# Reordering the first weight loads of a fused attention and MLP kernel, with a new issue order to go with it

## The chip, the cores and the metric

The kernel runs on one core of one Trainium2 chip. The metric is the device time of one execution in microseconds (us). The time before is the median of 11 executions.

## The reference

One input `x` (2048 tokens by 512 features, bfloat16) is layer-normed once to `xn`, and both branches read `xn`; the result is the sum of `x` and the two branches.

- Branch A: q, k and v are `xn @ wq`, `xn @ wk`, `xn @ wv`, split into 32 heads of 16 features. The 2048 tokens are cut into four segments of 512. In each segment every head does causal softmax attention inside the segment, and also reads a memory: with `phi(t) = t + 1` for positive t and `exp(t)` otherwise, the memory output is `phi(q) @ M / (phi(q) @ z)`. After the segment, `M += phi(k).T @ v` and `z += sum(phi(k))`. A sigmoid gate per head (`beta`) mixes the two, and the result goes through `wo`.
- Branch B: `silu(xn @ w1) @ w2` with 1792 hidden features.

```python
x = A_x
xn = _layernorm(x, axis=-1)
return x + _A_ref(xn, A_wq, A_wk, A_wv, A_wo, A_beta) + _B_ref(xn, B_w1, B_w2)
```

## The kernel before

The work is cut into tasks, and each task is a few instructions on one engine: a DMA issue on SyncE's queue (`"SP"`) or ScalarE's queue (`"ACTQ"`), matmuls on TensorE (PE), activations on ScalarE (ACT), vector work on VectorE (DVE), masks and small products on GpSimd (POOL). `Sched.add` makes a task with its engine, an assumed duration, an assumed delay until its result can be seen (`vis`), what it depends on and which buffers it takes. `Sched.run` then goes through the string `ORDER`, a list of task numbers written out by hand or by a search outside the kernel, and emits the tasks in that order. So the order of the instructions on every engine is `ORDER`; nothing is decided on the chip except the waits. `run` also keeps track of assumed times, and it uses them for one choice: which buffer of a ring a task gets.

The parts that matter here:

- **First loads.** `load_x` (line 369) and `load_w` (line 381) issue one DMA each. The first segment's four row tiles of `x` (128 tokens each) go out first, two on each queue. The weights `w_k` and `w_q` are loaded in two halves of 256 columns (256 KB each); the first halves serve the first two head groups. `w_v` is one load of 512 KB; `w_1` comes in two halves of 896 KB. The weights are loaded once and stay.
- **Warm-up.** 26 tasks of two small matmuls on an identity keep PE occupied until real work is there.
- **Layer norm of the first segment** (`ln`, line 546): for each row tile statistics on DVE (tile 2 on ACT), a power on POOL, the normalisation on DVE into `xn`, four transposes on PE (line 630) and a copy into `xnT` by ACT (line 643), or by DVE for tile 3 (line 645).
- **First projections.** `first_tile` (line 691) makes k and q of head group 0 in pieces, as row tiles come in: 128-column pieces for tiles 0 and 1, a 256-column piece for tiles 2 and 3. From a k piece ACT makes one half of `kB` (line 721) and DVE the other (line 723); DVE also keeps `kT` (line 731). `v_tile` (line 796) makes v for one row tile with four 512-column matmuls, and DVE evicts it to `V` (line 807).
- **The long middle.** `quad` (line 847) is one of 72 score groups: up to 16 small matmuls on 32-row tiles of PE write four PSUM banks `psS`, one ACT exponential over 2048 columns (line 870) reads them, and POOL masks the result (line 889). There is a single `psS`, so a score group waits for the exponential before it. Between two score groups PE does other work: projections, `w_1` and `w_2` matmuls, the probability-times-v products (`pv`), `w_o`.
- **The tail** (`tail`, line 1237): after the last score group the remaining `w_2` and `w_o` matmuls of the last segment, the last normalisation, and the stores.

All matmuls go through one helper, line 504 of the profile.

Of the kernel before, what the change touches and what calls it, by code (L numbers as in the profile page):

```python
# [64 lines left out]
1 3 5 14 27 0 2 53 63 28 29 15 30 31 32 64 33 54 34 4 35 36 58 55 37 38 39 40 41 42 65 59 60  # L65
43 44 45 66 70 46 71 47 56 57 48 49 50 51 67 61 62 72 52 96 109 16 6 110 68 69 97 111 7 8 9
10 98 73 74 18 114 115 99 17 116 11 112 113 100 117 19 147 101 102 184 118 103 136 129 12 130
185 131 187 148 149 132 137 150 104 105 138 188 189 268 269 270 139 76 75 271 272 13 151 133
280 106 281 282 283 140 77 284 78 84 124 273 186 192 125 107 285 126 127 193 143 81 128 274
275 82 276 277 119 120 121 122 21 123 135 196 168 278 279 169 170 108 83 171 194 172 286 287  # L70
288 289 163 164 197 142 141 190 200 79 298 299 300 301 292 80 293 290 294 85 295 291 134 86
199 201 302 87 165 89 166 167 204 152 153 154 296 297 155 328 198 329 330 202 331 205 156 179
303 203 90 180 173 332 333 88 208 209 181 191 195 182 159 144 145 304 158 305 157 160 183 220
222 221 210 212 213 306 307 161 352 353 354 355 356 214 215 358 308 309 382 383 384 385 216
217 310 311 312 386 206 313 314 363 364 146 315 428 429 430 357 431 175 226 227 211 365 366
367 432 316 317 318 319 207 218 320 22 321 371 372 373 374 230 671 219 672 673 674 223 231
375 228 176 234 177 433 225 368 235 675 229 434 224 91 435 436 420 437 174 421 390 391 178
376 392 393 237 92 238 239 322 323 324 325 326 422 394 443 444 445 236 446 377 676 423 424
241 242 243 438 439 327 440 369 447 441 20 240 359 334 335 336 337 442 338 339 677 678 246
247 401 402 403 404 405 232 340 360 341 342 343 346 347 348 349 93 450 23 233 250 679 361 244  # L80
680 344 345 350 351 94 245 409 410 411 412 413 251 248 370 262 264 254 487 252 488 406 407
489 572 162 451 452 453 454 455 456 457 458 459 460 461 462 463 464 465 466 397 255 256 253
580 490 263 467 491 258 259 257 492 362 681 493 494 517 689 690 691 692 693 495 249 496 571
587 588 398 497 498 260 499 261 579 581 682 518 519 694 500 425 501 520 399 400 582 589 387
521 583 522 523 524 388 590 591 265 266 449 469 584 448 683 592 684 685 573 686 687 525 389
595 526 527 596 267 695 696 697 24 698 502 574 426 427 585 528 529 530 531 599 688 503 594
504 593 505 597 701 702 703 704 506 408 470 471 699 700 395 577 578 507 600 602 705 508 603
872 873 874 586 601 509 875 510 511 512 532 706 604 533 416 534 598 606 535 607 536 605 513
608 514 515 623 417 475 610 611 537 476 538 516 713 25 575 576 378 472 539 624 26 540 714 715
379 380 719 716 541 477 612 615 720 396 721 717 718 625 478 722 542 543 876 544 616 545 755  # L90
756 757 479 619 758 836 837 838 546 839 483 614 723 724 759 831 731 481 613 732 609 733 734
618 620 629 832 735 833 707 474 415 840 708 736 841 842 617 621 418 853 834 835 473 709 710
843 844 482 630 711 622 633 846 712 847 848 634 468 845 849 850 626 627 637 414 638 381 812
813 814 815 743 766 744 628 635 480 767 768 769 641 485 762 486 484 553 554 555 877 816 559
556 745 560 631 878 746 561 642 562 645 640 770 557 774 636 737 775 738 776 760 739 777 747
748 740 547 643 563 548 646 879 649 564 778 632 549 550 741 742 644 817 1097 1098 647 1099
1100 650 551 565 566 567 648 1101 639 568 653 654 569 1102 95 665 419 771 761 804 805 806 667
807 781 763 881 880 764 808 725 882 779 657 658 998 666 656 1103 1104 1105 1106 1107 885 793
794 795 796 797 726 782 727 854 660 728 729 855 659 1108 652 661 662 655 1006 651 823 663 824
825 826 997 999 749 750 751 752 664 856 857 858 827 859 860 861 862 863 1013 864 865 730 785  # L100
786 787 788 866 867 753 754 798 868 869 1014 789 1127 1000 1128 870 1129 1130 1131 1017 765
1015 668 1005 913 914 1001 1002 780 669 887 772 1003 1004 915 852 1132 1007 1008 773 670 1018
1020 916 790 1011 917 888 1021 1012 1022 958 959 918 919 920 799 1024 960 921 922 923 961
1009 892 962 783 1025 800 801 1019 1133 924 925 1026 926 927 1010 1134 1135 1136 1137 963 964
1138 965 1029 1115 1116 1117 802 570 1118 1030 1109 1110 1111 1112 889 966 1113 851 1119 803
967 886 968 1114 1033 969 970 971 972 1016 1181 1023 1182 1031 1183 1196 1197 1198 894 1120
1199 1200 1034 1037 883 1188 1189 1190 1191 1032 1038 1192 1184 784 1028 1027 871 895 1185
1049 1051 1041 1050 893 1121 791 890 1122 928 929 1123 1040 819 1124 930 931 932 820 1035 792
1251 1042 1045 943 944 945 1036 933 934 946 1046 947 1039 948 1252 896 1043 1253 1055 821 935
1254 936 891 937 1125 938 1048 939 897 898 940 941 1126 901 949 950 1056 1059 1255 1044 1060  # L110
1047 1052 942 905 818 951 899 902 906 909 952 953 954 1053 884 1054 1187 1063 910 1157 1058
955 900 956 957 907 828 908 1061 829 1158 1159 1160 1203 1064 1065 1204 1161 1162 809 903 904
1067 1068 1246 1247 1248 1249 1205 1066 1206 1057 911 1241 1242 1250 1243 1139 1244 1071 1072
912 973 974 810 975 1140 976 1062 1070 1141 1207 830 1245 1142 1256 1257 1258 1259 1143 1069
811 1075 977 1073 1193 558 1144 1260 1211 1212 1213 1214 1076 1282 1283 1074 1284 1285 1186
1091 1079 1077 979 980 981 1215 982 1145 1208 1080 1082 1092 1093 1146 1081 1147 822 1148
1149 983 984 1150 985 986 1083 1218 978 1219 1220 1221 1222 1151 1152 1217 1153 1154 1286
1084 1194 1226 1078 1175 1155 1156 1087 1227 1228 1229 1287 1288 1176 1289 1230 1085 1177
1178 1233 1234 1235 1236 1237 1293 1088 1179 1407 1408 991 992 993 994 995 987 1163 1164 1165
1180 1166 1167 1086 1295 988 1411 1412 1089 989 1090 1094 1168 1201 1169 1170 1171 1172 1262  # L120
990 1096 1298 1264 1415 1265 1209 1266 1195 1493 1267 1494 1268 1495 1269 1496 1270 1173 1095
1297 1202 1271 1499 1500 1290 1501 1502 1416 1419 1299 1497 1174 1420 1353 1409 1417 1410
1354 1498 1272 1273 1355 1503 1504 1356 1357 1216 1291 1511 1512 1414 1421 1274 1275 1358
1276 1359 1422 1423 552 1513 1303 1277 1413 1424 1425 1514 1360 1304 1515 1305 1516 1261 1361
1529 1530 1531 1532 1533 1426 1418 1362 1278 1279 1280 1363 1427 1302 1296 1428 1430 1300
1364 1365 1292 1366 1505 1534 1301 1429 1506 1507 1367 1508 1517 1518 1519 1431 1323 1324
1520 1325 1326 1509 1510 1306 1311 1294 1443 1445 1432 1435 1327 1521 1522 1328 1436 1312
1444 1319 1329 1433 1330 1331 1332 1307 1308 1338 1339 1340 1341 1439 1437 1342 1343 1344
1320 1313 1438 1314 1434 1333 1334 1309 1440 1310 1345 1238 1335 1336 1449 1337 1346 1347
1321 1315 1316 1322 1239 1210 1441 1450 1442 1535 1536 1537 1538 1317 1318 1348 1349 1453  # L130
1368 1539 1263 1540 1452 1369 1370 1231 1371 1446 1240 1454 1455 1457 1372 1373 1374 1375
1447 1350 1351 1376 1223 1458 1377 1378 1379 1224 1225 1459 1460 1232 1461 1448 1456 1523
1380 1524 1381 1525 1462 1352 1526 1541 1451 1542 1527 1543 1544 1465 1466 1382 1577 1389
1390 1528 1391 1392 1383 1578 1579 1580 1384 1385 1463 1386 1469 1464 1545 1393 1559 1546
1394 1560 1561 1467 1562 1468 1485 1387 1486 1470 1473 1471 1472 1553 1554 1388 1555 1547
1548 1487 1563 1564 1581 1549 1550 1582 1556 1474 1551 1557 1552 1475 1401 1402 1403 1558
1477 1478 1592 1593 1565 1566 1567 1568 1404 1569 1405 1571 1572 1573 1574 1657 1481 1395
1396 1281 1583 1482 1479 1594 1658 1397 1597 1596 1398 1399 1480 1659 1660 1661 1662 1595
1663 1664 1599 1570 1621 1622 1623 1588 1400 1665 1666 1586 1476 1575 1667 1576 1484 1483
# [113 lines left out]
def kernel(  # L253
# [133 lines left out]
    def kv(w):  # L387
        return w.rearrange("(ko ki) n -> ki ko n", ki=P)
# [9 lines left out]
    C2, F2 = D // 2, F // 2  # L398
# [1014 lines left out]
```

## Time and profile before

| what | value |
|---|---|
| median of 11 runs | 226.56 us (224.83 to 227.66) |
| the profiled execution's own time | 225.19 us |
| its span, first to last instruction | 223.5 us |
| granted TensorE clock | 1.000 |
| PE busy | 213.9 us, 96% of the span, 2765 matmul records |
| DVE busy | 171.8 us, 77% |
| ACT busy | 181.1 us, 81% |
| POOL busy | 164.1 us, 73% |

The span is 1.7 us shorter than the profiled execution's own time, which holds what lies around the first and the last instruction. The profiled execution is 1.4 us faster than the median, so it is one of the quicker ones.

In the lines of the profile, `PE psS` is the score group and `PE ps` any other matmul; `SPq` and `ACTq` are DMA issues by the two queues' engines. "idle before <-X" is the time that the engine had stood idle and what ended it.

### The profile page before, as it was taken

Reading aid. Unit: us, or ns where it says so; the run is one execution under the profiler, and the core shown is the slowest. Engines: PE = TensorE matmul, PEld = TensorE weight load, DVE = VectorE, ACT = ScalarE, POOL = GpSimd, SP = SyncE. Lnnn points to the kernel's source line nnn. Section 1 sums busy time; section 2 is a strip of 40 time slices with the busy share of each in tenths; the row PEclk is TensorE's granted clock in tenths of the full one; section 3 lists DMA queues with packets and bytes.
Section 4 is the critical chain, followed back from the end, with each engine's and each line's share of the span. In section 5 each row is a group of like instructions: output and inputs, shape, how many; then the busy total and the mean of one; then the engine's idle time right before and its main releaser. Section 6 shows DMA issues by size and latency. Waiting matters only on the chain.

```text
span 223.5 us, 6732 instructions
## 1 busy us (share of the span) xinstructions
PE 213.9 (96%) x2765; PEld 102.8 (46%) x2800; DVE 171.8 (77%) x307; ACT 181.1 (81%) x166; POOL 164.1 (73%) x281
## 2 busy tenths in 40 slices
PE   7799999999999999999989999999999999999994
PEld 7544343534444444444533444344454535445553
DVE  3789985868979688779995849996747696685993
ACT  3589999999899987999979788899999798995100
POOL 2738899787789886698999879848858877648420
PEclk9999999999999999999999999999999999999999
DMA  5991844291145434150126722003245200023502
GB/s 159 353 286 28 165 75 147 62 329 15 23 34 119 91 72 112 32 168 27 26 50 136 145 78 66 0 15 88 73 110 126 76 21 3 13 73 108 163 14 94
DMA packets 30851, 21.10 MB, mean 94 GB/s; under 512 B 15972, under 2 KB 29924, under 8 KB 30820
## 3 DMA queue, kind: packets, MB, share of 16 engines
q1 hardware_dynamic: 30004, 20.14, 34.7%
q10 hardware_dynamic: 816, 0.52, 0.9%
q8 instruction: 22, 0.36, 0.7%
q14 instruction: 9, 0.07, 0.1%
HBM read 11.73 MB, written 2.64 MB: 64 GB/s over the span
## 4 chain that ended last, share of the span: by engine, by line
PE 85%; DMA 5%; POOL 3%; issue 3%; SPq 1%; DVE 1%; POOLq 0%
PE ps L504 72%; PE psS L504 13%; DMA w_k<-in_A_wk_dram 3%; POOL Pt L889 2%; DMA Dr<-dE 1%; DVE xn L617 1%; POOL kB L747 1%; SPq L373 1%; SPq L761 1%; DVE N L958 0%; POOL rstd L606 0%; POOL pkT L675 0%; PE ps L630 0%; DVE o_t L1308 0%; SPq L1234 0%
## 5 line engine op out<-in xcount | busy, mean ns | idle before, releaser
L870 ACT ACTIVATE Pt<-psS 128x2048 bf16<-128x2048 f32 x72 | 135.2, 1878 | 15.7 <-PE psS L504 12.4
L889 POOL TENSOR_SCALAR_AFFINE_SELECT Pt<-Pt 64x512 bf16<-64x512 bf16 (+1 forms) x144 | 90.5, 635 | 29.9 <-ACT Pt L870 24.0
L504 PE MATMUL ps<-xnT,w 128*128 128x512 bf16 x215 | 59.2, 380 | 0.5 <-issue 0.2
L504 PE MATMUL ps<-w,hT 128*128 128x512 bf16 (+1 forms) x199 | 50.9, 365 | 1.6 <-issue 0.6
L1178 DVE SCALAR_TENSOR_TENSOR hT<-hT,ps 128x512 bf16<-128x512 bf16 x56 | 37.7, 679 | 14.3 <-ACT hT L1174 14.0
L1174 ACT ACTIVATE hT<-ps 128x512 bf16<-128x512 f32 x56 | 32.8, 597 | 1.4 <-PE ps L504 1.1
L504 PEld LDWEIGHTS <-hT 128*128 128x128 bf16 x238 | 21.5, 98 | 23.0 <-issue 2.8
L504 PEld LDWEIGHTS <-w 128*128 128x128 bf16 x224 | 20.5, 98 | 24.4 <-issue 1.9
L504 PE MATMUL psS<-qT,kB 32*128 32x256 bf16 (+5 forms) x640 | 28.6, 262 | 0.3
L747 POOL TENSOR_SCALAR kB<-kT,pm 128x512 bf16<-128x512 bf16 x30 | 23.1, 772 | 1.3
L504 PEld LDWEIGHTS <-kB 32*128 32x128 bf16 x640 | 11.6, 92 | 26.1 <-issue 23.9
L504 PE MATMUL ps<-Pt,V 64*32 64x256 bf16 (+5 forms) x640 | 19.9, 260 | 0.0
L504 PE MATMUL ps<-xnT,w_k 128*128 128x512 bf16 (+2 forms) x71 | 18.1, 356 | 1.3 <-DMA w_k<-in_A_wk_dram 1.1
L504 PE MATMUL ps<-Pt,VS 64*32 64x256 bf16 (+5 forms) x640 | 18.8, 261 | 0.0
L1080 POOL TENSOR_TENSOR pq<-pq,Dr 128x512 bf16<-128x512 bf16 x12 | 14.3, 1189 | 5.2 <-DMA Dr<-dE 5.1
L504 PE MATMUL ps<-xnT,w_q 128*128 128x512 bf16 (+2 forms) x67 | 17.7, 355 | 0.2
L504 PEld LDWEIGHTS <-V 64*32 64x32 bf16 x640 | 14.2, 91 | 8.0 <-issue 2.8
L504 PE MATMUL ps<-w_v,xnT 128*128 128x512 bf16 x60 | 16.9, 380 | 0.3 <-issue 0.2
L504 PE MATMUL ps<-w_o,N 128*128 128x512 bf16 (+1 forms) x53 | 14.6, 368 | 0.3 <-issue 0.2
L504 PEld LDWEIGHTS <-VS 64*32 64x32 bf16 x640 | 12.9, 91 | 0.5 <-issue 0.5
L583 DVE BATCH_NORM_STATS2 st<-x_all 128x6 f32<-128x512 bf16 x15 | 10.2, 678 | 3.7 <-DMA x_all<-in_A_x_dram 3.7
L958 DVE CAST O<-ps 128x512 bf16<-128x512 f32 x15 | 10.3, 685 | 2.8 <-PE ps L504 2.8
(105 smaller groups left out, 254.7 us busy)
## 6 DMA issues: line engine op xcount, KB each, us to landing
w<-in_B_w_dram SPq DMA_DIRECT2D x4, 896.0 KB
VS<-V SPq DMA_DIRECT2D x8, 264.0 KB
R<-dR SPq DMA_DIRECT2D x15, 128.0 KB
out_dram<-o_t SPq DMA_DIRECT2D x15, 128.0 KB
Dr<-dE SPq DMA_DIRECT2D x12, 128.0 KB
x_all<-in_A_x_dram SPq DMA_DIRECT2D x2, 512.0 KB
N<-O SPq DMA_DIRECT2D x12, 64.0 KB
w_k<-in_A_wk_dram SPq DMA_DIRECT2D x2, 256.0 KB
```

The lines of the kernel that those rows point to most:

```text
L373: e.dma_start(out=x_all[:, c : c + n, :], in_=x_flat[t * P : (t + n) * P, :].rearrange("(j p) d -> p j d", p=P),)
L504: nc.tensor.matmul(o, lhsT=l, rhs=r, start=start, stop=stop, **k)
L583: nc.vector.bn_stats(out=b.tile[:], in_=xt(t))
L617: nc.vector.tensor_scalar(out=xb.tile[:], in0=xt(t), scalar1=mv[:, t, 0:1], scalar2=rstd[:, t, 0:1], op0=ALU.subtract, op1=ALU.mult,)
L747: nc.gpsimd.tensor_scalar(out=kB[u].tile[:, :, KB * r : KB * r + KB], in0=kT[u].tile[:].rearrange("p (a b) -> p a b", b=KB), scalar1=pm[:, ...
L761: nc.sync.dma_start(out=phiK_b[s].tile[:, :, dt * P : (dt + 1) * P], in_=pb.tile[:], transpose=True)
L870: nc.scalar.activation(out=pb.tile[:], in_=psS[:], func=AF.Exp, scale=SCALE)
L889: nc.gpsimd.affine_select(out=v, in_=v, compare_op=ALU.is_ge, fill=0.0, base=0, pattern=pat, channel_multiplier=-1,)
L958: nc.vector.tensor_copy(out=dst.tile[:, dt, :], in_=buf.tile[:])
L1080: nc.gpsimd.tensor_tensor(out=pb.tile[:], in0=pb.tile[:], in1=rb.tile[:], op=ALU.mult)
L1174: nc.scalar.activation(out=hb.tile[:], in_=b.tile[:], func=AF.Tanh, scale=0.5)
L1178: nc.vector.scalar_tensor_tensor(out=hb.tile[:], in0=hb.tile[:], scalar=1.0, in1=b.tile[:], op0=ALU.add, op1=ALU.mult)
```

## The change

The loads are the same loads with the same bytes. Before, SyncE's queue issued x0, x2, the first half of `w_k`, `w_v`, the first half of `w_1`, and ScalarE's queue x1, x3, the first half of `w_q`. Now SyncE's queue issues x0, x2, `w_v`, the first half of `w_1`, and ScalarE's queue x1, x3, the first half of `w_k`, the first half of `w_q`. The assumed delays of the first loads are altered with it, and the whole string `ORDER` is replaced, so that the instructions of all engines come in another order from the first projections to the end. No task is added or dropped. The pieces of k and q of head group 0 are grouped in the new order so that those of tiles 0 and 1 run one after the other.

```diff
 ORDER = """
-1 3 5 14 27 0 2 53 63 28 29 15 30 31 32 64 33 54 34 4 35 36 58 55 37 38 39 40 41 42 65 59 60
-43 44 45 66 70 46 71 47 56 57 48 49 50 51 67 61 62 72 52 96 109 16 6 110 68 69 97 111 7 8 9
...
+1 3 5 6 14 27 0 53 28 29 17 15 54 2 30 31 32 63 33 34 35 36 58 37 38 18 39 40 41 55 4 64 65
+42 43 44 45 46 47 48 59 60 56 7 49 50 51 61 70 52 66 67 57 114 71 115 62 116 117 68 69 97 72
...
-    load_x(0, 1, "SP", 0, 3.4)
-    load_x(1, 1, "ACTQ", 0, 3.55)
-    load_x(2, 1, "SP", 0, 3.6)
-    load_x(3, 1, "ACTQ", 0, 3.8)
+    load_x(0, 1, "SP", 0, 3.2)
+    load_x(1, 1, "ACTQ", 0, 3.25)
+    load_x(2, 1, "SP", 0, 3.35)
+    load_x(3, 1, "ACTQ", 0, 3.5)
...
-    ld_k = [load_w(*halves(w_k, A_wk, C2, 0), "SP", 0, 5.7)]
+    ld_v = load_w(w_v[:], kv(A_wv), "SP", 0, 6.0)
+    ld_k = [load_w(*halves(w_k, A_wk, C2, 0), "ACTQ", 0, 5.3)]
     ld_q = [load_w(*halves(w_q, A_wq, C2, 0), "ACTQ", 0, 6.4)]
-    ld_v = load_w(w_v[:], kv(A_wv), "SP", 0, 7.5)
-    ld_1 = [load_w(*halves(w_1, B_w1, F2, 0), "SP", 0.1, 9.5)]
-    load_x(4, 2, "SP", 0.2, 9.8)
-    load_x(6, 2, "SP", 0.2, 10.0)
-    ld_1.append(load_w(*halves(w_1, B_w1, F2, 1), "SP", 0.3, 12.0))
-    ld_k.append(load_w(*halves(w_k, A_wk, C2, 1), "SP", 0.3, 12.5))
-    ld_q.append(load_w(*halves(w_q, A_wq, C2, 1), "SP", 0.3, 12.5))
+    ld_1 = [load_w(*halves(w_1, B_w1, F2, 0), "SP", 0.1, 9.3)]
+    load_x(4, 2, "SP", 0.2, 9.9)
+    load_x(6, 2, "SP", 0.2, 10.2)
+    ld_1.append(load_w(*halves(w_1, B_w1, F2, 1), "SP", 0.3, 12.1))
+    ld_k.append(load_w(*halves(w_k, A_wk, C2, 1), "SP", 0.3, 12.4))
+    ld_q.append(load_w(*halves(w_q, A_wq, C2, 1), "SP", 0.3, 12.6))
```

The first real matmuls on PE, in words. Before: k of tile 0, q of tiles 0 and 1, transposes of tile 2, k of tile 1, transposes of tile 3, most of v of tile 0, q and k of tiles 2 and 3, the first score group. After: v of tile 0, transposes of tile 2, k of tiles 0 and 1, transposes of tile 3, q of tiles 0 and 1, k and q of tiles 2 and 3, v of the next tile, the first score group.

## The prediction

> **What bounds the kernel now.** I read the page first: busy times, then the chain that ended last.
>
> ```profile
> PE 213.9 (96%) x2765; PEld 102.8 (46%) x2800; DVE 171.8 (77%) x307; ACT 181.1 (81%) x166; POOL 164.1 (73%) x281
> PE 85%; DMA 5%; POOL 3%; issue 3%; SPq 1%; DVE 1%; POOLq 0%
> ```
>
> TensorE is busy all the time and carries 85% of the chain. A busy PE may still be waiting inside, so next I read the timeline of PE around 80 us, where nothing special happens:
>
> ```profile
> 78.01 0.40 PE L504 MATMUL psS<-qT,kB 32*128 32x256 bf16 x12
> 78.34 0.82 PE L504 MATMUL ps<-xnT,w 128*128 128x512 bf16 x3
> 79.00 1.03 PE L504 MATMUL ps<-w,hT 128*128 128x512 bf16 x4
> 79.86 0.81 PE L504 MATMUL ps<-xnT,w_k 128*128 128x512 bf16 x3
> 80.60 0.40 PE L504 MATMUL psS<-qT,kB 32*128 32x256 bf16 x12
> ```
>
> From score group to score group it is 2.59 us, with ten 512-column matmuls between. Successive 512-column matmuls start 0.216 us apart (78.34 to 79.00 for three, with rounding), so the score group with its change of tile shape takes 2.59 - 2.16 = 0.43 us. I applied this to all 71 intervals (0.43 us for a group, 0.216 us for each 512 columns, 1.16 us for a product of probabilities and v with its change of shape). It gives 186.0 us from the first score group (12.21 us) to the last (201.11 us); measured is 188.9. So PE truly waits for 2.9 us in the whole middle, mostly in single waits like this one, the largest:
>
> ```profile
> 113.56 2.53 PE L504 MATMUL ps<-w,hT 128*128 128x512 bf16 x11 [0.62 <-DVE N L958]
> ```
>
> The middle is bound by matmuls. What a reordering can win or lose is the start, up to the first score group, and those waits.
>
> The start, from the timeline of the first 24 us:
>
> ```profile
> 1.71 0.46 ACTq L384 DMA_DIRECT2D w_q<-in_A_wq_dram  x1
> 1.74 0.44 SPq L384 DMA_DIRECT2D w_k<-in_A_wk_dram  x1
> 2.22 0.59 SPq L384 DMA_DIRECT2D w_v<-in_A_wv_dram  x1
> 2.86 0.51 SPq L384 DMA_DIRECT2D w<-in_B_w_dram  x1
> ...
> 8.65 0.40 PE L504 MATMUL ps<-xnT,w_k 128*128 128x128 bf16 x4 [1.12 <-DMA w_k<-in_A_wk_dram]
> 8.75 0.41 DVE L617 TENSOR_SCALAR xn<-x_all,mv,rstd 128x512 bf16<-128x512 bf16 x1 [0.44 <-POOL pm L422]
> ...
> 10.14 0.82 PE L504 MATMUL ps<-w_v,xnT 128*128 128x512 bf16 x2
> ...
> 12.21 0.39 PE L504 MATMUL psS<-qT,kB 32*128 32x512 bf16 x4
> ...
> 12.69 1.87 ACT L870 ACTIVATE Pt<-psS 128x2048 bf16<-128x2048 f32 x1
> ```
>
> PE stands idle for 1.12 us until `w_k` is there at 8.65, then is nearly full to 12.21. The last tile's `xn` is ready only at 9.16 (8.75 + 0.41), whatever the weights do.
>
> How full the DMA engines are meanwhile, from the windows of one microsecond (last two columns: busy share of the 16 engines, GB/s):
>
> ```profile
> 4.00:5.00 1.00, 1.00 (x12) 1.00 (x10) 0.93 (x4) 0.26 (x1) 0.08 (x1) 1.00 0.64 176
> 5.00:6.00 1.00, 0.97 (x11) 0.79 (x8) 0.93 (x4) 0.97 (x3) 0.64 (x2) 1.00 0.79 207
> 6.00:7.00 1.00, 0.84 (x12) 0.67 (x12) 0.75 (x5) 0.73 (x3) 0.93 (x2) 1.00 1.01 301
> 7.00:8.00 1.00, 0.51 (x6) 0.34 (x6) 0.93 (x4) 0.72 (x2) 0.12 (x1) 1.00 1.08 357
> ```
>
> While two queues move rows of 512 bytes (halves of `w_k` and `w_q`, 4 to 6 us) the engines have slack; from 6 us they are full.
>
> **The change, part by part.**
>
> *Issues.* ScalarE issues one DMA more (0.46 us), so its table load ends near 3.9 instead of 3.5; its first work waits for x until 4.74 anyway: nothing. SyncE issues one less, so `w_v` goes out at 1.74 and `w_1` at 2.22. If the cover to 4.74 were gone, 0.46 us.
>
> *When the weights land.* `w_v` is needed first now. Lower bound: the bytes of x, `w_v` and half of `w_k` (1.31 MB) have passed by 7.1 us at the rates of the windows; with 0.4 us from last packet to first user (`w_k`: last packet record 8.2, first matmul 8.65) that is 7.5. Upper bound: where it lands now, 10.1. I take 8.4, nearest to `w_k`'s 8.65, whose place it takes; a few engines ran about 2 us behind the others there, and they would hold this load too. `w_q` now lies behind `w_k` and beside `w_1`, which is issued earlier: between 8.3 (its last packet now is at 7.9) and 10.8 (all of x, the three weights and an equal share of `w_1`, 1.83 MB, by 8.5, plus 0.4 and those 1.9 of delay). I take 9.6.
>
> On the Trainium skill, page "DMA: Bandwidth & Descriptors", section "Issuing engines are not separate DMA queues": transfers from all queues run on the same 16 engines, and another queue saves only issue time. By that rule the move to ScalarE's queue would win only the 0.46 us of issue on SyncE. The trace speaks partly against it, since the engines were only 64 to 79% busy from 4 to 6 us; were the rule the whole truth, my sum below would be some 0.1 to 0.5 us worse.
>
> *From `w_v` to the first score group.* PE in its new order: v 4 x 0.216 = 0.86, transposes 0.22, k 8 x 0.055 = 0.44, transposes 0.22, q 0.44, then k of tiles 2 and 3 0.43: 2.6 us. Behind that ACT makes its half of the second `kB` (0.48), DVE `kT` (0.41) and, in DVE's new order only then, its half of the first `kB` (0.48), with 0.3 us of hand-overs: 1.7. So the first score group starts at `w_v` + 4.3, and not before 12.3, because the last `xn` (9.16), transposes, copy, k and the same DVE chain end there. With 8.4: 12.7, against 12.21: +0.5. The other price: `w_q` + 2.5 = 12.1, hidden unless it lands after 10.2. The 0.63 us exponential for `phi` stands ahead of the first big exponential on ACT now; it needs `kT` (11.9 to 12.2) and ends about when the score group does, so it costs 0 to 0.2 there.
>
> *What PE has done by then.* Counted in both orders: three more 512-column matmuls before the first score group, and three more after the last. So the 71 intervals hold six fewer: 186.0 - 1.3 = 184.7 us, the tail has 0.65 us more. The number of changes of tile shape is the same within two (171 and 173 changes). Sum: +0.5 - 1.3 + 0.65 = -0.15 us.
>
> *Waits in the middle.* Early on the new order has DVE tight. After the first score group DVE does a `kB` half, a V eviction, three row statistics (0.86 each), `kT`: that `kT` ends 4.35 us after the start of the group, while PE wants its bank at 4.2; and the glu that frees another bank ends at 9.75 against 9.6. With hand-overs 0.45 us of waits where the trace of before has none (its first seven intervals are 2.45 to 2.81 as computed). For the rest of the middle I can read no wait from the orders alone; I leave the 2.9 us as they are, between 1.6 (its three largest gone) and 5.8 (double). The ACT load between two exponentials is at most two small activations in both orders. The tail's order has PE filled while DVE does its two reciprocals (3.36 us) as now; 0 to 0.5 us.
>
> Sum: -0.15 + 0.45 = +0.3, with no gain. On the profiled execution 225.19 + 0.3 = 225.5; on the median of the runs, which is 1.4 us above the profiled one, 226.9; I say 226.7, as the early DVE wait partly overlaps the later start. About 0.5% (1.1 us) is what a measurement can tell from no change; this is inside.
>
> **The rivals.**
>
> *Slower: the load that PE now stands behind is late.* PE's queue is in order, and the largest of the three weights is at its head; transposes, k and q wait behind `w_v`. For it: one slow engine holds the whole load, `w_k` and `w_q` had that in this trace, and `w_v` has twice the bytes. Against: `w_v` is out 0.48 us earlier than before. Price: with `w_v` at 10.1 the first score group is at 14.4, +2.2, less 0.65, plus 0.45: +2.0, 228.5. It decides from `w_v` at 9.3 on (13.55 is the first score group that costs 1.1 us in all); `w_q` after 11.0 does the same.
>
> *Faster: the order has fewer waits.* `w_v` lands at 7.5, the first score group at its floor of 12.3: +0.1 - 0.65 = -0.55; no early DVE wait, and the three largest waits of the middle (0.68, 0.34 and 0.30 us) are gone: -1.3. 224.7. For it: these waits belong to the old order. Against: every order has its own.
>
> *Nothing at all:* weights are hidden behind the last tile's `xn` at 9.16 anyway, the order is as good as the old one: 226.5. It falls together with the forecast.
>
> **The numbers.** No change within 0.5% (225.43 to 227.69), forecast and "nothing" together: 0.43, own range 225.6 to 227.6. Slower: 0.37, since late weights and new waits both lie there. Faster: 0.20. The range runs from 224.9, which leaves out about half of the faster case, to 228.6, just above the price of the slower rival.
>
> **What would show it.** Right: `w_v` the releaser of the first real matmul, near 8.4; the first score group at 12.5 to 13.0; the last one 188 us later; short waits of PE on DVE between 15 and 25 us. Wrong: a first score group before 12.2 or after 13.5, or waits in the middle that sum to under 1.6 or over 5.8 us.

## The result, and the profile after

The changed kernel takes 228.08 us in the median of 12 runs (227.31 to 229.38), the kernel before 225.96 in 47 runs beside it: ratio 1.0091, 95% interval 1.0067 to 1.0115. It is slower by 2.1 us. The profiled execution took 227.56 us, its span is 225.8 us, the granted clock 1.0. Ratios compare runs within 1.5% of each kernel's fastest; medians and ranges are of all runs. The forecast of 226.7 was too low; the range up to 228.6 held the time, and what came true is the slower rival, by its second clause: "`w_q` after 11.0 does the same".

The page of after, busy times and chain:

```profile
PE 214.9 (95%) x2769; PEld 103.9 (46%) x2800; DVE 173.0 (77%) x307; ACT 181.6 (80%) x166; POOL 161.6 (72%) x281
PE 64%; POOL 15%; DVE 6%; issue 5%; ACT 4%; DMA 4%; ACTq 1%; POOLq 0%; DVEq 0%
PE ps L504 53%; PE psS L504 11%; POOL Pt L889 8%; DMA w_q<-in_A_wq_dram 4%; ACT Pt L870 3%; DVE xn L617 2%; POOL kB L747 2%; POOL pq L1080 1%; POOL rstd L606 1%; POOL pq L675 1%; DVE hT L1178 1%; DVE pq L681 1%; POOL Mbf L997 0%; DVE pkT L681 0%; ACT hT L1174 0%
```

TensorE works as long as before (214.9 against 213.9 us) in a span that is 2.4 us longer. The load that the chain names is another one now: before, the first half of `w_k` stood there with 3%, now the first half of `w_q` with 4%. It was issued last of the first loads on ScalarE's queue, and the timeline of the start shows what it did:

```profile
1.71 0.43 SPq L384 DMA_DIRECT2D w_v<-in_A_wv_dram  x1
1.73 0.46 ACTq L384 DMA_DIRECT2D w_k<-in_A_wk_dram  x1
2.19 0.51 SPq L384 DMA_DIRECT2D w<-in_B_w_dram  x1
2.21 0.58 ACTq L384 DMA_DIRECT2D w_q<-in_A_wq_dram  x1
...
8.09 1.02 PE L504 MATMUL ps<-w_v,xnT 128*128 128x512 bf16 x3 [0.31 <-DMA w_v<-in_A_wv_dram]
...
9.18 0.61 PE L504 MATMUL ps<-xnT,w_k 128*128 128x128 bf16 x8
...
11.70 0.62 PE L504 MATMUL ps<-xnT,w_q 128*128 128x128 bf16 x8 [1.69 <-DMA w_q<-in_A_wq_dram]
...
14.26 0.40 PE L504 MATMUL psS<-qT,kB 32*128 32x512 bf16 x4 [0.21 <-DVE kB L723]
```

`w_v` is early (8.09 us), `w_k` is there when it is wanted (9.18), and then PE stands 1.69 us before `w_q`, with everything else queued behind. The first score group is at 14.26 us, before at 12.21. In the windows of one microsecond the engines are full from 5 us on, where before they had slack until 6:

```profile
5.00:6.00 1.00, 1.00 (x13) 1.00 (x11) 0.91 (x6) 0.69 (x2) 0.96 (x3) 1.00 1.08 362
10.00:11.00 1.00, 0.01 (x1) 0.00 (x0) 0.76 (x2) 0.01 (x1) 0.85 (x5) 1.00 1.12 347
```

(The first column behind the window is its length, then PE, PEld, DVE, ACT, POOL, the clock, the busy share of the DMA engines, GB/s.) At 10 to 11 us PE works 0.01 us while 347 GB/s pass.

The span falls into three parts, cut at the starts of the first and the last score group (us):

| kernel | first score group | from there to the last | behind it | span |
|---|---|---|---|---|
| before | 12.21 | 188.89 | 22.37 | 223.5 |
| after | 14.26 | 188.78 | 22.80 | 225.8 |

So +2.05 at the start, -0.11 in the middle although it has six matmuls less, +0.43 in the end.

**Who passes beside `w_q`.** Counting the DMA packet records of after by queue and size: from 7.5 to 9.0 us ScalarE's queue moved 245 packets of 512 bytes (`w_q`), SyncE's queue 235 of 1792 bytes (`w_1`) and 10 others. From 5.0 to 6.5 us, with `w_v` on SyncE's queue, it was 311 packets of 512 against 307 of 1024 and 35 of 1792. So the two queues moved about as many packets as each other, though one's were 2 or 3.5 times as long, and beside `w_1` the bytes were shared 23 to 77, not equally. The records don't name the engine, so single turns can't be seen. On the Trainium skill, page "DMA: Bandwidth & Descriptors", section "Queues, rings and completion order": each engine goes round between the queue rows that have work, at the granularity of packets. There a packet is a whole group of descriptors, typically 9 to 17; here a packet is one record, as long as one row. Near-equal counts agree with the rule, and can't tell turns of one row from turns of equal groups.

### The profile page after: what moved, and what is told of

Same layout as the page of the kernel before. It is cut to its first block, busy times and chain, and to the rows that moved or that the text cites. A ratio compares the mean times of both kernels' runs of the same rounds, so it can differ in the third digit from the quotient of the medians.

```text
span 225.8 us, 6734 instructions
## 1 busy us (share of the span) xinstructions
PE 214.9 (95%) x2769; PEld 103.9 (46%) x2800; DVE 173.0 (77%) x307; ACT 181.6 (80%) x166; POOL 161.6 (72%) x281
## 4 chain that ended last, share of the span: by engine, by line
PE 64%; POOL 15%; DVE 6%; issue 5%; ACT 4%; DMA 4%; ACTq 1%; POOLq 0%; DVEq 0%
PE ps L504 53%; PE psS L504 11%; POOL Pt L889 8%; DMA w_q<-in_A_wq_dram 4%; ACT Pt L870 3%; DVE xn L617 2%; POOL kB L747 2%; POOL pq L1080 1%; POOL rstd L606 1%; POOL pq L675 1%; DVE hT L1178 1%; DVE pq L681 1%; POOL Mbf L997 0%; DVE pkT L681 0%; ACT hT L1174 0%
## 5 line engine op out<-in xcount | busy, mean ns | idle before, releaser
L747 POOL TENSOR_SCALAR kB<-kT,pm 128x512 bf16<-128x512 bf16 x30 | 22.3, 749 | 0.9
L504 PE MATMUL ps<-xnT,w_q 128*128 128x512 bf16 (+2 forms) x70 | 17.0, 355 | 1.7 <-DMA w_q<-in_A_wq_dram 1.7
L504 PEld LDWEIGHTS <-V 64*32 64x32 bf16 x640 | 14.3, 91 | 8.4 <-issue 3.6
L1080 POOL TENSOR_TENSOR pq<-pq,Dr 128x512 bf16<-128x512 bf16 x12 | 14.2, 1190 | 0.2
L807 DVE CAST V<-ps 128x512 bf16<-128x512 f32 x16 | 11.0, 685 | 4.1 <-PE ps L504 3.9
L504 PE MATMUL ps<-w_o,N 128*128 128x512 bf16 (+1 forms) x54 | 14.0, 367 | 0.2 <-issue 0.2
L583 DVE BATCH_NORM_STATS2 st<-x_all 128x6 f32<-128x512 bf16 x15 | 10.2, 679 | 4.4 <-DMA x_all<-in_A_x_dram 4.4
```

Source lines behind the costliest of these rows:

```text
L504: nc.tensor.matmul(o, lhsT=l, rhs=r, start=start, stop=stop, **k)
L583: nc.vector.bn_stats(out=b.tile[:], in_=xt(t))
L747: nc.gpsimd.tensor_scalar(out=kB[u].tile[:, :, KB * r : KB * r + KB], in0=kT[u].tile[:].rearrange("p (a b) -> p a b", b=KB), scalar1=pm[:, ...
L807: nc.vector.tensor_copy(out=bass_pair(o), in_=i)
L1080: nc.gpsimd.tensor_tensor(out=pb.tile[:], in0=pb.tile[:], in1=rb.tile[:], op=ALU.mult)
```

## The experiments

Theories: (A) `w_q` lands late because it lies behind `w_k` and takes turns with `w_1`'s long rows; (B) the new order loses by itself. The first two kernels do one half of the change each; the next two keep the new order and change what passes beside or ahead of `w_q`.

**Loads only.**

```diff
-    ld_k = [load_w(*halves(w_k, A_wk, C2, 0), "SP", 0, 5.7)]
+    ld_k = [load_w(*halves(w_k, A_wk, C2, 0), "ACTQ", 0, 5.7)]
```

in the kernel before, with `w_k`'s issue placed right behind x in `ORDER`; nothing else moves on any engine.

> The old issue order with the new placement of the loads (w_v behind x on SyncE's queue, w_k and w_q both on ScalarE's). Theory A: the loss sits in the landing of w_q, which lies behind w_k and takes turns, packet against packet, with w_1's longer rows. Then w_q is usable at 11.7 us as in the changed kernel, the first score group follows q of tiles 0 and 1 by 3.2 us as before (8.88 to 12.21, less 0.15 of waiting): 14.9 us, 2.7 later than before; 228.7 us, ratio about 1.012. Theory B: the loss sits in the new order (its chain at the start, its waits), the loads are indifferent: first score group within 0.5 of 12.2, ratio 1.000 to 1.002.

Measured: 232.49 us, ratio 1.0237 (1.0177 to 1.0297): worse than either theory. The start:

```profile
9.71 0.40 PE L504 MATMUL ps<-xnT,w_k 128*128 128x128 bf16 x4 [2.33 <-DMA w_k<-in_A_wk_dram]
12.57 1.03 PE L504 MATMUL ps<-xnT,w_q 128*128 128x128 bf16 x8 [2.47 <-DMA w_q<-in_A_wq_dram]
```

Theory A's wait is there (`w_q` usable at 12.57, expected 11.7), and a second thing: eight 128-column matmuls take 1.03 us in place of 0.62. The windows show why (the clock is the third number from the end):

```profile
11.00:12.00 1.00, 0.00 (x0) 0.00 (x0) 0.00 (x0) 0.00 (x0) 0.05 (x1) 0.80 1.09 363
12.00:13.00 1.00, 0.42 (x5) 0.43 (x6) 0.00 (x0) 0.00 (x0) 0.00 (x0) 0.50 1.07 377
...
18.00:19.00 1.00, 1.00 (x9) 0.39 (x8) 0.18 (x1) 0.32 (x1) 0.00 (x0) 0.79 0.00 0
```

After only 0.4 us of matmuls since 7.4 us the granted clock fell to half, from about 11.6 to 18.4 us (0.80 and 0.79 are the parts of those two windows), so the first score group came at 18.57. All 6 runs show it (mean clock over the span 0.985 or 0.993).

**Order only.** The changed kernel with `w_k` on SyncE's queue ahead of `w_v`, as before; the assumed delays are adjusted so that every other instruction and buffer is the changed kernel's.

```diff
-    ld_v = load_w(w_v[:], kv(A_wv), "SP", 0, 6.0)
-    ld_k = [load_w(*halves(w_k, A_wk, C2, 0), "ACTQ", 0, 5.3)]
-    ld_q = [load_w(*halves(w_q, A_wq, C2, 0), "ACTQ", 0, 6.4)]
+    ld_v = load_w(w_v[:], kv(A_wv), "SP", 0, 5.5)
+    ld_k = [load_w(*halves(w_k, A_wk, C2, 0), "SP", 0, 5.3)]
+    ld_q = [load_w(*halves(w_q, A_wq, C2, 0), "ACTQ", 0, 6.9)]
```

> The new issue order with the old placement of the loads (w_k, then w_v on SyncE's queue, w_q on ScalarE's). Theory A: the new order needs w_v first, and with the old placement that is usable at 10.0 to 10.1 us. First score group at w_v + 4.3 = 14.3 us, the same total as the changed kernel by another road: 228.1 us, ratio 1.009 (1.006 to 1.011); the releaser of the first real matmul is w_v. The middle stays at about 189.0 us and what follows the last score group at 22.6. Theory B (the new order is as good as the old one by itself): ratio 1.000. Theory C (the new order loses all by itself, in the middle): first score group before 13 us and yet ratio 1.009.

Measured: 227.94 us, ratio 1.0047 (1.0009 to 1.0085), first score group 13.53, middle 188.65, end 22.80.

```profile
8.80 1.02 PE L504 MATMUL ps<-w_v,xnT 128*128 128x512 bf16 x3 [1.03 <-DMA w_v<-in_A_wv_dram]
...
13.53 0.40 PE L504 MATMUL psS<-qT,kB 32*128 32x512 bf16 x4 [0.34 <-DVE kB L723]
```

`w_v` was usable at 8.80, earlier than I had read from before (there PE came to it only at 10.14). Theory A had it at 10.0 to 10.1 and the first score group at 14.3, which did not come; the interval leaves out theory B's 1.000 and theory A's 1.009, not the lower end of A's range, 1.006. The new order loses at the start even so. 6 of 12 runs had the lower clock (0.992 or 0.993); no profile of one was kept that would show why. From `w_v` to the first score group it is 4.73 us, not 4.3.

**x ahead of `w_1`.** The changed kernel with the issue of `w_1`'s first half moved behind the two loads of x4 and x6 in `ORDER`.

> The changed kernel, but the two loads of x for the second segment (512 rows-per-partition packets of 1024 bytes) go out on SyncE's queue ahead of the first half of w_1 (packets of 1792 bytes). w_q's place in its own queue is untouched. Theory A, turns packet against packet: w_q's 512 packets pass beside 512 packets of x (0.52 MB) in place of the 512 packets of w_1 (0.92 MB): 0.4 MB less ahead of its end, at 0.35 MB per us 1.1 us earlier: usable at 10.6, first score group 13.15, 227.0 us, ratio 1.0045. Theory A', equal shares by bytes: w_q has the same share whatever lies beside it: 11.7 us, ratio 1.009. Theory B, the order is the cause: ratio 1.009 as well, but then with an earlier w_q.

Measured: 228.34 us, ratio 1.0061 (1.0025 to 1.0097); `w_q` usable at 11.40, first score group 13.97. The interval holds 1.0045 and 1.009, so the times tell nothing apart. `w_v` too was 0.76 us later in this execution (8.85 against 8.09). The trace speaks partly against theory A: it had `w_q` usable at 10.6, and 11.40 is nearer to the 11.7 of equal shares by bytes. The counts are not equal either. From 7 to 8 us ScalarE's queue moved 320 packets of 512 bytes and SyncE's 169 of 1024, which is nearly equal in bytes. Why is open, so equal turns are not a rule for every pair of loads.

**Pair on SP.** The changed kernel with `w_k` and `w_q` on SyncE's queue ahead of `w_1`, and `w_v` on ScalarE's.

```diff
-    ld_v = load_w(w_v[:], kv(A_wv), "SP", 0, 6.0)
-    ld_k = [load_w(*halves(w_k, A_wk, C2, 0), "ACTQ", 0, 5.3)]
-    ld_q = [load_w(*halves(w_q, A_wq, C2, 0), "ACTQ", 0, 6.4)]
+    ld_v = load_w(w_v[:], kv(A_wv), "ACTQ", 0, 6.0)
+    ld_k = [load_w(*halves(w_k, A_wk, C2, 0), "SP", 0, 5.3)]
+    ld_q = [load_w(*halves(w_q, A_wq, C2, 0), "SP", 0, 6.4)]
```

> The changed kernel with its order, but w_k and w_q lie on SyncE's queue ahead of w_1, and w_v on ScalarE's queue behind x. Nothing of w_1 can then pass before w_q. Theory A: all three weights have landed when about 1.57 MB have passed, near 7.8 us, usable by 8.2 to 8.8; no matmul of the start waits for w_q any more; the first score group is bound by the last tile's normalised x and comes at 12.3 to 12.7 us, 1.6 to 1.9 us before the changed kernel's: 226.3 us, ratio 1.0015 (1.000 to 1.004). Middle about 189.0, end 22.6, as in the changed kernel. Theory B (the new order costs the 2 us by its own waits): ratio 1.009.

Measured: 226.97 us, ratio 1.0008 (0.9977 to 1.0039), against 1.0091 for the changed kernel with every instruction of PE, DVE and POOL the same. Theory A's number was 1.0015, theory B's 1.009: with the new order kept, another placement of these loads gives the 2 us back. No profile of one of its runs at full clock was kept, so how these start isn't seen. The profiled execution is the one of 12 at a lower clock (0.993) and is not typical: `w_v` came at 10.12 there, 2.69 us after PE's last matmul, and the clock was 0.50 from 9.9 to 13.3 us:

```profile
10.12 0.59 PE L504 MATMUL ps<-w_v,xnT 128*128 128x512 bf16 x1 [2.69 <-DMA w_v<-in_A_wv_dram]
```

**Loads only, filled.** A test of the clock: loads-only with 10 matmuls on the identity ahead of the first k piece and 20 ahead of the first q piece.

```diff
+            nf = {("k0", 0): 10, ("q0", 0): 20}.get((label, js[0]), 0)
-            def f(c=c, o=o):
+            def f(c=c, o=o, nf=nf):
+                for _ in range(nf):
+                    mm(psS[:, 3, 0:P], ident[:], ident[:], True, True)
```

> Loads-only again (old order, new placement of the loads), with 30 more small matmuls on the identity: 10 ahead of the first k piece, 20 ahead of the first q piece, so that TensorE is not idle while it waits for w_k and w_q. Each took 0.108 us in the warm-up of before (4.55 us for 42), so 1.1 and 2.2 us, less than the two waits of loads-only (2.33 and 2.47 us). Theory G: in loads-only the granted clock fell to 0.50 from 11 to 18 us because TensorE had done next to nothing from 7.4 to 11 us, and this, not the loads, makes the part of the loss above 2.7 us. Then the clock stays at 1.00, the first score group comes 3.2 us after w_q (some 15.0 to 15.8), and 232.5 becomes about 229.2 us, ratio 1.012 (1.009 to 1.015). Rival: the clock has another cause and stays at 0.985 over the span; ratio 1.024 as in loads-only, or more by up to 3.2 us for the added matmuls.

Measured: 229.61 us, ratio 1.0172 (1.0125 to 1.022), clock 1.0 in all 4 runs. With more work all four runs (229.31 to 229.89) are below all six of loads-only (230.53 to 233.18), 2.9 us in the median, and the first score group comes at 16.43 in place of 18.57, though `w_q` was later: the clock is the second part of loads-only's loss. The rest is late loads, more than expected (1.009 to 1.015, first score group 15.0 to 15.8):

```profile
9.91 0.40 PE L504 MATMUL ps<-xnT,w_k 128*128 128x128 bf16 x4 [1.51 <-DMA w_k<-in_A_wk_dram]
13.09 0.62 PE L504 MATMUL ps<-xnT,w_q 128*128 128x128 bf16 x8 [1.66 <-DMA w_q<-in_A_wq_dram]
```

**Full rows.** A sharper test of the turns: the changed kernel, with packets of twice the length beside `w_q`.

```diff
-    ld_1 = [load_w(*halves(w_1, B_w1, F2, 0), "SP", 0.1, 9.3)]
+    ld_1 = [load_w(w_1[:], kv(B_w1), "SP", 0.1, 9.3)]
-    ld_1.append(load_w(*halves(w_1, B_w1, F2, 1), "SP", 0.3, 12.1))
+    ld_1.append(A("SP", 0.5, lambda: None, due=0.3, vis=12.1, label="w"))
```

> The changed kernel, but the first load of w_1 takes whole rows (512 rows of 3584 bytes, 1.75 MB) in place of half rows (512 of 1792 bytes), and the second load of w_1 issues nothing. Everything else is the changed kernel's. Theory A, turns packet against packet: the 512 packets of w_q have 512 packets of 3584 bytes beside them, 0.9 MB more ahead of its end, 2.6 us at 0.35 MB per us: w_q usable at about 14.3 in place of 11.7. TensorE then idles 4 us, the granted clock falls to 0.50 for some 3.4 us (1.7 us more): first score group about 17 to 18.5, 230.7 to 232.5 us, ratio 1.02 to 1.028. Theory A', equal shares by bytes: w_q lands where it did, 228.1 us, ratio 1.009; the same if long rows are cut into packets no longer than w_1's half rows.

Measured: 230.83 us, ratio 1.0246 (1.0186 to 1.0307), all 4 runs at a clock of 0.985 or 0.993.

```profile
13.12 0.62 PE L504 MATMUL ps<-xnT,w_q 128*128 128x128 bf16 x8 [2.51 <-DMA w_q<-in_A_wq_dram]
...
16.52 0.61 PE L504 MATMUL psS<-qT,kB 32*128 32x512 bf16 x4
```

The same loads in the same places; only the neighbour's rows are longer, and `w_q` is 1.4 us later than in after. Equal shares by bytes would have left it at 11.7. Since a landing moves between executions (see below), the times count for more: all four runs (230.36 to 233.06) are above all twelve of after (227.31 to 229.38). From 7.5 to 9.0 us the records show 130 packets of 512 bytes beside 135 of 3584 and 42 of 1024, 11 to 89 in bytes; from 9.0 to 10.5 us 86 beside 155. Turns are only roughly equal here; that some engines were through with `w_q` by then would explain it, and is not shown. `w_q` is 1.2 us earlier than expected: up to its last packet 3.38 MB had passed, 0.52 MB more than in after and not 0.9, at 377 to 411 GB/s from 8 to 13 us and not 350.

**One step of the order.** The largest wait of the new order's middle is of the kind that the prediction showed for before: TensorE waits for a bank that VectorE has not evicted, as VectorE is busy with a normalisation. From the timeline of after:

```profile
67.32 0.87 DVE L617 TENSOR_SCALAR xn<-x_all,mv,rstd 128x512 bf16<-128x512 bf16 x1
...
68.26 0.68 DVE L958 CAST O<-ps 128x512 bf16<-128x512 f32 x1
...
68.99 1.02 PE L504 MATMUL ps<-xnT,w 128*128 128x512 bf16 x4 [0.77 <-DVE O L958]
```

In `ORDER` task 583 (this normalisation) goes behind 266 (the second eviction). First with the loads of pair-on-SP:

> The kernel with the new order and w_k, w_q on SyncE's queue ahead of w_1 (pair-on-SP), with one step moved on VectorE: the normalisation that stands ahead of the two evictions of a probabilities-times-v product (67.32 us in the changed kernel's trace) goes behind them. Theory: the 0.77 us wait of TensorE for O there (the largest wait of the new order's middle) shrinks to 0.2 or less and nothing else comes late: 0.5 to 0.75 us less than pair-on-SP, ratio 1.0008 - 0.003 = 0.998. The middle is 188.1 us. Rival: the wait turns up at the next group that needs a bank or the normalised x: middle 188.6 to 188.8, ratio 1.001. Its profile should also show what pair-on-SP is when w_v is not late: w_v and w_q usable by 8.8, first score group 12.3 to 13.0.

Measured: 226.34 us, ratio 1.0002 (0.9963 to 1.0041), 4 of 12 runs with a lower clock. The interval around that wait is 2.73 us in place of 3.52, and the middle of the profiled execution 187.58 in place of 188.63. The ratio holds both 0.998 and the rival's 1.001.

```profile
9.19 1.02 PE L504 MATMUL ps<-w_v,xnT 128*128 128x512 bf16 x4 [1.73 <-DMA w_v<-in_A_wv_dram]
...
13.92 0.40 PE L504 MATMUL psS<-qT,kB 32*128 32x512 bf16 x4 [0.34 <-DVE kB L723]
```

PE doesn't wait for `w_q` here, but `w_v` is late now (9.19), so the start expected at 12.3 to 13.0 did not come: the first score group is only 0.34 us ahead of after's. Then with the changed kernel's own loads:

> The changed kernel, loads and all, with only the one step moved on VectorE (the two evictions ahead of the normalisation, as in pair-and-evict). Theory: the 0.77 us wait of TensorE for O is gone in the 21st interval (3.52 us in every kernel with the new order and this step unmoved), and the start is the changed kernel's: w_q usable at 11.4 to 12.0, first score group 14.0 to 14.6. 0.4 to 0.8 us less than the changed kernel (part of it may come back as other waits): ratio 1.0063 (1.004 to 1.008). Rival: all of it comes back later in the middle: middle 188.8 us as before the move, ratio 1.009. If the first score group is before 13 us in this profile, the landing of w_q differs from run to run by more than the 2 us that it cost.

Measured: 227.52 us, ratio 1.0079 (1.0050 to 1.0108), middle 187.81, the interval 2.74. The step is worth its 0.8 us in that place (full-rows, with the step unmoved, has 2.60 us there, not 3.52, but 1.1 and 0.3 us more in two intervals just ahead, with waits for N and hT); of the median, which it was to shorten by 0.4 to 0.8, the intervals settle nothing. The profiled execution is worth more than the comparison:

```profile
8.60 1.02 PE L504 MATMUL ps<-w_v,xnT 128*128 128x512 bf16 x4 [0.99 <-DMA w_v<-in_A_wv_dram]
...
10.52 0.61 PE L504 MATMUL ps<-xnT,w_q 128*128 128x128 bf16 x8
...
13.34 0.40 PE L504 MATMUL psS<-qT,kB 32*128 32x512 bf16 x4 [0.34 <-DVE kB L723]
```

No wait for `w_q`: its last packet ended at 9.18 us here, at 11.07 in after. Its span, 223.9 us, is the shortest of the 8 runs; the other seven lie at 225.6 to 226.7. The packet records tell how: by 4.5 us ScalarE's queue had moved 267 packets of 512 bytes here, and 20 in after. Here ScalarE's queue was through with its x first: `w_k` began at 3.66 us and `w_v` at 3.93; in after it was `w_v` at 3.52 and `w_k` at 3.90. Where that queue gets ahead, fewer of its packets are left beside `w_1`. Of the profiles with the changed placement of the loads, after, x-ahead, loads-only and loads-filled show fewer than 25 such packets by 4.5 us, full-rows 141. Which queue is through with x first, and why, is open.

**Filled, with the pair.** Pair-and-evict with `f_w` of the last warm-up task making 16 matmuls in place of 2.

> Pair-and-evict (new order, w_k and w_q on SyncE's queue, the two evictions ahead of the normalisation) with 14 more warm-up matmuls at the end of the warm-up, in the idle time before w_v: about 0.065 us each by the filled kernel's rows (20 in 1.28 us), 0.9 us of 1.7. Theory G: 4 of the 12 runs of pair-and-evict show a granted clock of 0.984 to 0.992 and spans 1 to 4 us longer; with TensorE kept at work up to about 8.4 us they go, and nothing else changes: all clocks at 0.998 or above, median about 225.8 us, ratio 0.997 (0.994 to 0.999). Rival: the drops come from a w_v that lands after 10 us, which the filler doesn't cover: still 2 to 4 of 12 low, ratio 1.000.

Measured: 227.33 us, ratio 1.0038 (1.0010 to 1.0066). No run is below 0.998, as theory G says, yet the median is not lower. The profiled execution has its first score group at 12.90 (`w_v` at 8.17) and a middle of 188.47, 0.9 more than pair-and-evict, with no releaser that I can name; it is the quickest of its 12 runs, so it does not stand for the median. Why the median rose is open.

**The kernel before, with its own largest wait moved.** Task 1001 (the normalisation at 111.16 us) goes behind 669 (the eviction of N); the transpose by DMA that needs it follows it. Loads and all else are the old ones.

> The kernel before, with one step moved on VectorE: the normalisation at 111.16 us (1.75 us there) goes behind the eviction of N that TensorE's largest wait of the middle (0.62 us at 113.56) is for. Theory: that wait is gone, the middle is 188.3 us in place of 188.9; 0.4 to 0.6 us less, ratio 0.998 (0.996 to 0.9995). Rival: the long normalisation makes the next step late by the same amount: ratio 1.000. This is the candidate that beats both kernels.

Measured: 225.29 us, ratio 0.9981 (0.9949 to 1.0013). The wait is gone:

```profile
113.64 2.55 PE L504 MATMUL ps<-w,hT 128*128 128x512 bf16 x11
```

The profiled execution has one stop of 1.85 us at 124.53 put down to issue; it is why its middle is 190.21. Then with 8 more warm-up matmuls:

> The kernel before with N's eviction ahead of the long normalisation, and 8 more warm-up matmuls at the end of the warm-up (0.5 us of the 1.1 us idle before w_k). Theory: as without them, 0.4 to 0.6 us under the kernel before, from the 0.62 us wait of TensorE that is gone; the filler takes away the rare runs at a lower clock (2 of the 23 of before in the last set). Ratio 0.998 (0.996 to 0.9995), median about 225.5 us. Rival: w_k is there early in some runs (7.5 us in the last profile) and the filler then delays it by 0.5 us: ratio 1.000.

Measured: 225.72 us against 226.66 for before beside it, ratio 0.9957 (0.9924 to 0.9990). By this ratio it is 0.1 to 0.8% faster than before, and so than after. The mean of all twelve runs, 226.48 against 226.71, shows next to nothing, as 4 of them still had a clock of 0.992 and took 226.58 to 230.12 us. Neither the step nor the filler is shown to be the reason. The profile's middle is 189.84, longer than before's 188.89; its start is early (first score group 11.55). And it has a stop ahead of the same matmuls as the form without the filler (that form first, then this one):

```profile
124.53 1.67 PE L504 MATMUL ps<-xnT,w_k 128*128 128x512 bf16 x7 [1.85 <-issue]
122.53 1.67 PE L504 MATMUL ps<-xnT,w_k 128*128 128x512 bf16 x7 [1.02 <-DVE acc L1203]
```

These matmuls read the transposed `xn` of the next segment. In both profiles the last of its four transposes is issued 1.2 us ahead of the score group before the stop, in before 2.0 us. So the expectation's rival, that the moved normalisation makes a later step late, may well be true; loads-filled, with the step unmoved, has its last transpose at 1.05 us and a wait of 0.33 in that place, so it is not shown.

## Why the prediction was right in its range and wrong in its sum, step by step

- **The signs and the range.** `w_v` did release the first real matmul, at 8.09. By its own signs the prediction was wrong: the first score group, 14.26, is later than the 13.5 that it named. The range held the time because it reached to the slower rival's price; no change within 0.5%, the likeliest case at 0.43, did not come.
- **Which step failed: the landing of `w_q`.** Taken 9.6 us with an upper end of 10.8, "an equal share of `w_1`"; measured 11.70 in after, 13.12 beside longer rows. In after the share was about equal in packets, not in bytes. `w_q`'s 512 packets then pass beside all 512 of `w_1`'s half: 2.49 MB (x, the three weights, the whole half of `w_1`) up to its end in place of 1.83, or 1.9 us at 0.35 MB per us. The records agree: at `w_q`'s last packet 518 packets of `w_1` had passed, and 0.36 MB of the loads behind it, 2.86 MB in all. The price that I had written, hidden until 10.2 and then one for one, held: after's 11.70 gives 1.5 us, and 14.26 is 1.44 above `w_v` + 4.73.
- **`w_v`:** taken 8.4, measured 8.09, and 8.60 to 8.85 in the three other profiled kernels that keep the new order and this place for it. The mechanism was right. Its old landing was read as 10.1 from the moment PE came to it. A first use is only an upper bound, but a near one here: in the trace of before its last packet ended at 9.46, in order-only, with the same place for `w_v`, at 8.39, 0.41 before its first user. Most of the difference to 8.80 is between executions.
- **From `w_v` to the first score group:** 4.3 taken; 4.73 in order-only, 4.73 in pair-and-evict and in its filled form, 4.74 in the last run. PE has 0.3 us of short gaps around q that I had not seen. In the profiles with `w_q` in time the new order's first score group is at 12.90, 13.34, 13.53 and 13.92, in the old order's with the old loads at 11.55, 12.21 and 12.47. So part of the loss at the start, 0.6 us of the 2.05 in after (8.09 + 4.73 against 12.21), is not `w_q`.
- **Matmuls moved:** three more behind the last score group, +0.65: the end is 22.80 to 22.86 us in every profile of the new order and 22.14 to 22.16 in four of the old, exactly that; the profile of before happened to have 0.2 more. Of the six fewer in the middle less is to be seen: 187.6 to 189.3 in the new order's profiles (188.6 to 189.3 without the moved step), 188.9 to 190.5 in the old one's.
- **Waits in the middle:** left at 2.9, measured 188.78 - 184.7 = 4.1, inside the stated 1.6 to 5.8. The early one that I expected on DVE (0.45) shows as 0.2 for `kT` at 25 us; the largest is another, 0.77 for O.
- **Sum:** +0.3 predicted; the spans show +2.05 - 0.11 + 0.43 = +2.37, the medians +2.1. Of the +2.05, 1.44 is `w_q`. Pair-on-SP's median gives back nearly all of the change (1.0008), more than this term; what else its runs win is not seen in a profile.
- **The rival** "slower" had the place right (PE's queue in order behind one late load) and the price (228.5 against 228.08), but put the chance on `w_v`: the price was worked out for `w_v` at 10.1 us, and that it fits with `w_v` at 8.09 and `w_q` at 11.70 is partly luck. Its argument against, that `w_v` goes out earlier, was true and beside the point.
- **The rule weighed** ("Issuing engines are not separate DMA queues": another queue saves only issue time) spoke against the change, and it was the better guide, though the 0.1 to 0.5 us that I took from it is less than the 2.1 measured; it says nothing of how two queues share. I let 64 to 79% busy engines between 4 and 6 us speak for spare room; the second load of the pair went out of that room into `w_1`'s.
- What stays open: the run-to-run start of ScalarE's queue, and the medians of the last new-order kernels, which lie above what their profiles show, and the unequal counts in x-ahead.

## What to carry to other kernels

In after, loads-only and loads-filled two queues on the same engines moved about as many packets as each other from 5 to 9 us: a load of short rows beside one of long rows got the small part of the bytes (23% in after). So put the load that is needed first ahead of the long rows in the same queue, and count the neighbour's packets as well as its bytes. See which load becomes the last one then: with `w_k` and `w_q` on SyncE's queue it was `w_v`, whose first matmul came between 8.17 and 10.12 us. Read when a load lands from a wait that it ends, or from its last packet, not from its first use, and expect the landing to move: `w_q`'s last packet came at 9.18 and at 11.07 us with the same loads. For TensorE with a long idle wait ahead of it, price the clock as well as the wait.

## What the hardware showed that was not expected

The granted clock. Where TensorE had been idle, or nearly so, for 2.4 to 4 us, the clock fell to 0.50 and stayed there for 3.4 us (pair-on-SP 9.9 to 13.3; full-rows 14.2 to 17.6) or 6.8 us (loads-only 11.6 to 18.4). In full-rows PE had waited 2.51 us, and the clock fell 1.1 us after the matmuls had come back:

```profile
13.00:14.00 1.00, 0.88 (x12) 0.85 (x13) 0.15 (x1) 0.00 (x0) 0.00 (x0) 1.00 1.11 342
14.00:15.00 1.00, 1.00 (x7) 0.65 (x6) 0.55 (x2) 0.56 (x2) 0.00 (x0) 0.60 1.14 301
```

Filling the wait with 30 small matmuls on the identity kept the clock at 1.0 in all 4 runs of loads-filled. The Trainium skill, page "TensorE: Matmul & The Clock Gate", section "What's actually happening", has a free-running window of 3.4 us and a half clock after an idle one. The clock's records agree: their changes in the first 20 us are 3.41 us or twice that apart. What counts is the work within such a stretch, and this is why the fall in full-rows came late. PE was busy for 0.97 of the 3.41 us before the fall in pair-on-SP (6.46 to 9.87), for 0.40 in loads-only (8.18 to 11.60) and for 1.09 in full-rows (10.79 to 14.21). It was busy for 1.68 in pair-and-evict (6.71 to 10.12), for 1.90 and 1.76 in loads-filled and for 2.23 and 2.36 in after, and the clock stayed. So a stretch need not be wholly idle, as "an idle one" might suggest; in these profiles the limit lies between 1.1 and 1.7 us of work.
